# ScalarE and VectorE repeat 60 heads of a layer in loops, three heads a turn, beside TensorE

## The chip, the core and the metric

The kernel runs on one core of a Trainium2 chip. Its engines are TensorE (PE, with its weight loads as PEld), VectorE (DVE), ScalarE (ACT), GpSimd (POOL) and SyncE (SP), which issues all DMA transfers of tensors. The engines run on their own and wait for each other by semaphores. The metric is the time of one execution on the device in microseconds (us), lower is better.

## The reference, cut to what matters

Two layers, each an attention over a key-value cache and then a small mixer and MLP; one token for each of two batch entries. The weights are the same in both layers, and so are the caches: each layer reads all of K and V (2 x 32 heads x 16384 positions x 128, bfloat16, 268 MB each).

```python
def _A_ref(x, k_cache, v_cache, wq, wo):
    q = (x @ wq).reshape(B, Sq, H, Dh).transpose(0, 2, 1, 3)
    scores = jnp.einsum("bhqd,bhkd->bhqk", q, k_cache) * (Dh ** -0.5)
    p = _softmax(scores, axis=-1)
    o = jnp.einsum("bhqk,bhkd->bhqd", p, v_cache)
    return o.transpose(0, 2, 1, 3).reshape(B, Sq, H * Dh) @ wo
...
x = x + _A_ref(_layernorm(x), A_k_cache, A_v_cache, A_wq, A_wo)
x = x + _B_ref(_layernorm(x), B_w1, B_w2, B_w3, B_w4)
# and both lines once more
```

`_B_ref` is a layer norm, two 576x576 products around a shift along the sequence, and an MLP of 576 to 4608 to 576.

## The kernel before, in words

A "head" below is one of the U = 64 pairs of batch entry and head. K and V of one head are one tile each of 128 partitions x 32 KB (4 MB). The memory `mem` has six slots for such tiles; the plan in `plan_all` gives each tile its slot and its order in SP's queue: K of head s+1, then V of head s, and so on. The last two heads of the first layer and K of one more stay in memory and come first in the second layer (`order`, CARRY = 2). A transfer is issued when its slot is free: class `Store` records on which instructions it has to wait, and SP issues strictly in order (L98).

The whole program is recorded first as a list of operations per engine (class `Graph`); each names what it reads and writes, and `_waits` works out which other operations it must wait for, leaving out what another wait covers. `emit` then writes the engines' instructions. Operations of TensorE inside a range noted with `loop` are written once, as a hardware loop of turns; the waits of such a loop go to semaphores of its own (`own`), which each turn takes down again at its end (`_turn`). A loop cannot hold a wait for a DMA semaphore, whose value grows from turn to turn; so for TensorE, GpSimd waits for the tile (`landed`, `relay`, L177) and passes it on. VectorE and ScalarE are written out in full, instruction by instruction, for all heads, with one counting semaphore (`done`).

`attention` is the pass over heads, s = 0 to 63, each in eight chunks c (32 of the 64 blocks of each half of K go this way, `PB` = 32):

- TensorE transposes the eight blocks of chunk c (L852, into `tps`), ScalarE copies them out (L862, `kt`), and TensorE multiplies them with the query two chunks later (L872, scores into `sps`; LEAD = 2). So in chunk 0 of head s TensorE does the transposes of chunk 0 and the scores of chunk 6 of head s-1.
- VectorE does the other half of the scores itself, in four pieces at c = 0, 2, 4, 6: a product of K with the query in all partitions (L886, into `prod`) and a sum (L890, into `s_dve`). The first piece waits for the K tile's DMA.
- At c = 2 VectorE copies the output of head s-2 away (`keep_o`, L923) and takes the maxima of head s-1 (L897 to L901); GpSimd takes the maximum over partitions (L904); at c = 4 ScalarE writes the exponentials of head s-1 and their sums into columns of `l1` and `l2` (L912 to L917).
- From c = 4 to 7 TensorE multiplies the exponentials of head s-1 with V, a quarter at a time (`pv`, L941).
- At c = 6 the query of head s+1 is prepared: VectorE copies its column (L816) and scales a diagonal matrix with it (L818), TensorE spreads it over the partitions (L821), ScalarE copies it out (`qb`, L824).

After the last head `normalize` adds `l1` and `l2`, sums over partitions and scales the output; then come the products with wo, w3 and w4, whose weights take the places of the last tiles. In the first layer TensorE's loop is s = 1 to 60, in the second s = 4 to 63.

Of the kernel before, what the change touches and what calls it, by code (L numbers as in the profile page):

```python
# [16 lines left out]
class Op:  # L17


    __slots__ = ("eng", "fn", "deps", "waits", "needed", "own", "val", "sem", "sig", "pos", "know", "relay")  # L20

    def __init__(self, eng, fn, sig=None):
        self.eng, self.fn, self.sig = eng, fn, sig
        self.deps, self.waits = [], []
        self.needed = self.own = self.relay = False
        self.val = self.sem = self.know = None
# [6 lines left out]
class Graph:  # L33
# [5 lines left out]

    ENGS = ("sync", "scalar", "tensor", "vector", "gpsimd")  # L40

    def __init__(self, nc):
        self.nc = nc
        self.ops = {e: [] for e in self.ENGS}
        self.all = []
        self.writer = {}
        self.readers = {}
        self.dma_sems = {}
        self.dma_count = {}
        self.loops = []  # L50
# [25 lines left out]
    def op(self, eng, fn, reads=(), writes=(), sig=None):  # L76
        return self._add(Op(eng, fn, sig), reads, writes)
# [24 lines left out]

    def loop(self, first, turns):

        n = len(self.ops["tensor"]) - first
        assert n % turns == 0
        self.loops.append((first, n // turns, turns))
# [19 lines left out]
    def emit(self):  # L127
        nc = self.nc
        self._waits()
        pe = self.ops["tensor"]  # L130
        turn = {}
        for first, n, turns in self.loops:
            for i in range(first, first + n * turns):
                turn[i] = (first, n, (i - first) // n)
        for o in self.all:
            for d in o.waits:
                d.needed = True
                if o.eng == "tensor" and o.pos in turn and d.sem is None:
                    d.own = True
        for first, n, turns in self.loops:  # L140
            for i in range(n):
                same = [pe[first + i + n * t] for t in range(turns)]
                assert all(o.sig is not None and o.sig == same[0].sig for o in same), [o.sig for o in same]
                some = any(o.needed for o in same)
                for o in same:
                    o.needed = some
        done = {e: nc.alloc_semaphore(f"done_{e}") for e in self.ENGS if e != "sync"}
        own = {e: nc.alloc_semaphore(f"own_{e}") for e in self.ENGS if e not in ("sync", "tensor")}
        for o in self.all:
            if o.relay:  # L150
                o.own = o.needed = True
        for e in self.ENGS:
            n = {True: 0, False: 0}
            for o in self.ops[e]:
                if o.sem is None and o.needed:
                    n[o.own] += 1
                    o.val = n[o.own]
        for o in self.all:
            for d in o.waits:
                assert not d.own or o.eng == "tensor", (o.eng, d.eng)  # L160

        def wait(eng, need, seen):
            for (s, mine), v in need.items():
                if seen.get((s, mine), -1) < v:
                    eng.wait_ge(self.dma_sems[s] if s in self.dma_sems else (own if mine else done)[s], v)
                    seen[s, mine] = v

        def needs(o):
            need = {}
            for d in o.waits:  # L170
                k = (d.sem if d.sem is not None else d.eng, d.own)
                need[k] = max(need.get(k, 0), d.val)
            return need

        def emit_op(eng, e, o):
            if o.relay:
                eng.sem_inc(own[e], 1)  # L177
                return
            ins = o.fn(eng)
            if o.sem is None and o.needed:  # L180
                ins.then_inc((own if o.own else done)[e], 1)

        def runner(e):
            def run(eng):
                seen = {}
                for o in self.ops[e]:
                    wait(eng, needs(o), seen)
                    emit_op(eng, e, o)
            return run

        def run_pe(eng):
            seen, taken = {}, {}
            i = 0
            loops = {first: (n, turns) for first, n, turns in self.loops}
            while i < len(pe):
                if i in loops:
                    n, turns = loops[i]
                    taken = self._turn(eng, pe, i, n, turns, taken, wait, needs, emit_op, own)
                    seen = {k: v for k, v in seen.items() if not k[1]}
                    i += n * turns  # L200
                    continue
                o = pe[i]
                need = {k: v - (taken.get(k[0], 0) if k[1] else 0) for k, v in needs(o).items()}
                wait(eng, need, seen)
                emit_op(eng, "tensor", o)
                i += 1

        with nc.Block() as block:
            for e, sect in (("sync", block.sync), ("scalar", block.scalar), ("tensor", block.tensor),
                            ("vector", block.vector), ("gpsimd", block.gpsimd)):  # L210
                if self.ops[e]:
                    sect(run_pe if e == "tensor" else runner(e))

    def _turn(self, eng, pe, first, n, turns, taken, wait, needs, emit_op, own):

        table = [[needs(pe[first + t * n + i]) for i in range(n)] for t in range(turns)]
        assert all(k[1] for row in table for need in row for k in need), "a wait that no loop can hold"
        top = [{} for _ in range(turns)]
        for t, row in enumerate(table):
            for need in row:  # L220
                for (s, _), v in need.items():
                    top[t][s] = max(top[t].get(s, 0), v)
        step = {s: top[-1][s] - top[-2][s] for s in top[-1]}
        assert all(s in step for row in top for s in row)
        rel = []
        for i in range(n):
            need = {}
            for t in range(turns):
                for (s, m), v in table[t][i].items():
                    r = v - t * step[s] - taken.get(s, 0)  # L230
                    assert need.get((s, m), r) == r, (i, pe[first + i].sig, t, s, r, need)
                    need[s, m] = r
            rel.append(need)
        for s, v in step.items():
            assert max(need.get((s, True), 0) for need in rel) >= v, (s, v)
        me = eng.engine
        with self.nc.Fori(0, turns, 1, engines=OrderedEngineSet([me]), head_slot={me: 0}):
            seen = {}
            for i in range(n):
                wait(eng, rel[i], seen)  # L240
                emit_op(eng, "tensor", pe[first + i])
            for s, v in step.items():
                eng.sem_inc(own[s], -v)
        return {**taken, **{s: taken.get(s, 0) + v * turns for s, v in step.items()}}
# [60 lines left out]
class KB:  # L305
# [38 lines left out]
    def _alloc(self):  # L344
# [10 lines left out]
        self.qb = [sb(f"qb{i}", [128, 128], BF16) for i in range(2)]  # L355
        self.p = [sb(f"p{i}", [128, self.NB], BF16) for i in range(self.NS)]
        self.s_dve = [sb(f"s_dve{i}", [128, 2 * (self.BP - self.PB)], FP32) for i in range(2)]
        self.q_f = sb("q_f", [128, U], FP32)
        self.q_col = sb("q_col", [128, self.NS], BF16)
        self.mx = sb("mx", [128, 5, 4], FP32)  # L360
        self.l1 = sb("l1", [128, U], FP32)
        self.l2 = sb("l2", [128, U], FP32)
        self.o_acc = sb("o_acc", [128, U], FP32)
        self.otn = sb("otn", [128, U], BF16)
# [4 lines left out]
        self.rows = self.prod[:, 1024:1024 + self.D]  # L369
        self.x = sb("x", [128, KT, B], FP32)  # L370
# [10 lines left out]
        self.hg = [sb(f"hg{i}", [128, KT * NL * B], FP32) for i in range(2)]  # L381
# [110 lines left out]
    def dv(self, fn, reads=(), writes=()): return self.g.op("vector", fn, reads, writes)  # L492
    def act(self, fn, reads=(), writes=()): return self.g.op("scalar", fn, reads, writes)
# [55 lines left out]
    def layer(self, l):  # L549
# [6 lines left out]
        self.rows_projection("wo", l, lambda k: self.otn[:, k * self.B:(k + 1) * self.B], "otn")  # L556
# [182 lines left out]
    def attention(self, l):  # L739
        U, LEAD, NS = self.U, self.LEAD, self.NS  # L740
        o = self.order(l)
        pe = self.g.ops["tensor"]
# [3 lines left out]
        enter = self.CARRY + 2 if l else 1  # L746
        leave = enter + NS * ((U - enter) // NS)
        leave = min(leave, U) if l else leave - NS
# [4 lines left out]
        for s in range(U + 1):  # L753
            if s == enter:
                first = len(pe)
            if s == leave:
                self.g.loop(first, (leave - enter) // NS)
            if s < U and not self.kept(l, s):
# [3 lines left out]
            for c in range(2 * n):  # L762
                h = c // n
                if s < U:
                    u = o[s]
                    self.transposes(l, s, u, c)
                    self.evacuate()
                    pend.append((s, u, c, self.chunk))
                    self.chunk += 1
                while pend and (len(pend) > LEAD or s == U):  # L770
                    self.scores(*pend.pop(0))
                if s < U:
                    if c == 0 and prompt and s >= 1:
                        self.q_broadcast(o[s + 1], s + 1)
                    if c % n in (0, 2):
                        self.dots(l, s, u, h, c % n // 2)
                    if c == 2 * n - 2 and not prompt and s + 1 < max(U, leave + 1):
                        self.q_broadcast(o[min(s + 1, U - 1)], s + 1)
# [8 lines left out]
                elif s >= 1:  # L787
                    if c == LEAD:
                        if s >= 2:
                            self.keep_o(s - 2, o[s - 2])  # L790
                        self.softmax_max(l, s - 1, o[s - 1])
# [5 lines left out]
            if prompt:  # L797
                while pend:
                    self.scores(*pend.pop(0))
                if s >= 1:  # L800
                    self.keep_o(s - 1, o[s - 1])
                self.softmax_max(l, s, o[s])
        self.keep_o(U - 1, o[U - 1])
# [10 lines left out]
    def q_broadcast(self, u, s):  # L814
        i = s % self.NS
        self.dv(lambda e: e.tensor_copy(out=self.q_col[:, i:i + 1], in_=self.q_f[:, u:u + 1]),  # L816
                reads=["q_f"], writes=[("q_col", i)])
        self.dv(lambda e: e.tensor_scalar(out=self.diag[:, :], in0=self.ident[:, :], scalar1=self.q_f[:, u:u + 1],  # L818
                                          scalar2=None, op0=ALU.mult), reads=["ident", "q_f"], writes=["diag"])
# [230 lines left out]
```

## Time and profile before

| | |
|---|---|
| time, median of 3 runs | 2573.72 us (2573.01 to 2574.47) |
| profiled execution, own time | 2572.36 us |
| its span, first to last instruction | 2570.6 us |
| granted TensorE clock, mean | 0.571 |
| busy: PE, DVE, ACT, POOL | 63%, 74%, 47%, 6% |
| DMA: bytes, mean rate over the span | 1097 MB, 427 GB/s |
| K tile, V tile: median time from issue to landing | 41.2 us, 49.9 us |

The page cuts the span into 40 slices of 64 us and gives busy shares and DMA rate for each. The sum of waits tells for each engine and line what it waited for ("us in total, times, longest us"). In a timeline the columns are start, length, engine, line, operation, output and input, count, and in brackets the idle time ahead of it with what ended it. "SPq" is an instruction that SP issues. The length of an SP row that stands for several transfers is from the first to the last of them.

### The profile page before, as it was taken

The page shows a single profiled execution, that of the slowest core. Times are in us where ns is not written, and L with a number is a line of the kernel's source. Part 1 is how long each engine was busy: PE and PEld are TensorE (multiplying, and loading weights), DVE is VectorE, ACT ScalarE, POOL GpSimd, SP SyncE. Part 2 cuts the span into 40 slices and gives each one's busy share as a digit, 9 for nine tenths or more (in the row PEclk, how much of TensorE's full clock was granted, in tenths as well). Part 3 has the DMA queues.
Part 4 walks back from the last instruction along what each step waited for, and adds up shares of the span by engine and source line. Part 5 has one row for each costly group of instructions (what it writes and reads, how often), then busy time and mean ns, then how long its engine had stood idle before and what let it go on. Part 6 is the DMA issues. An engine that isn't in the chain of part 4 may idle for free.

```text
span 2570.6 us, 73557 instructions
## 1 busy us (share of the span) xinstructions
PE 1612.5 (63%) x34309; PEld 1575.9 (61%) x34309; DVE 1897.4 (74%) x1920; ACT 1203.8 (47%) x1816; POOL 158.9 (6%) x149
## 2 busy tenths in 40 slices
PE   4666566666656666666667766666666665666665
PEld 4666566666656656565557766656666665665665
DVE  5877777776777777678559977777777777777773
ACT  3544444444544444454335554444454444444442
POOL 0000000000000000000000000000000000000000
PEclk8555555555565555555556555555555555555555
DMA  9999999999999999999999999999999999999999
GB/s 408 431 432 431 430 432 431 431 431 433 431 431 433 432 432 432 432 432 430 389 405 430 431 431 431 432 432 432 432 432 431 431 432 432 431 432 431 431 421 349
DMA packets 58873, 1097.27 MB, mean 427 GB/s; under 512 B 4778, under 2 KB 23342, under 8 KB 23854
## 3 DMA queue, kind: packets, MB, share of 16 engines
q1 hardware_dynamic: 58798, 1096.33, 99.9%
q8 instruction: 40, 0.66, 0.1%
q14 instruction: 35, 0.29, 0.0%
HBM read 1096.30 MB, written 0.00 MB: 426 GB/s over the span
## 4 chain that ended last, share of the span: by engine, by line
DMA 66%; DVE 26%; PE 5%; issue 2%; SPq 0%; ACT 0%; DVEq 0%; POOL 0%; POOLq 0%
DMA mem<-in_A_k_cache_dram 60%; DVE s_dve L890 16%; DVE prod L886 9%; DMA mem<-in_A_v_cache_dram 4%; PE mps L941 2%; PE tps L852 2%; DMA mem<-in_B_w_dram 1%; DMA mem<-in_A_wo_dram 1%; PE sps L821 1%; SPq L98 0%; DMA mem<-in_A_wq_dram 0%; DVE diag L818 0%; PE sps L629 0%; PE mps L700 0%; DVE mx L901 0%
## 5 line engine op out<-in xcount | busy, mean ns | idle before, releaser
L862 ACT ACTIVATE kt<-tps 128x1024 bf16<-128x1024 bf16 x1026 | 1036.9, 1024 | 885.9 <-PE tps L852 868.8
L890 DVE TENSOR_REDUCE s_dve<-prod 128x16 f32<-128x2048 bf16 x512 | 1168.3, 2282 | 17.6
L852 PE MATMUL tps<-ident,mem 128*128 128x128 bf16 x8208 | 1001.8, 300 | 181.1 <-POOLq L177 178.2
L886 DVE TENSOR_TENSOR prod<-mem,qb 128x2048 bf16<-128x2048 bf16 x512 | 625.4, 1221 | 544.7 <-DMA mem<-in_A_k_cache_dram 528.7
L941 PE MATMUL mps<-p,mem 128*128 128x1 bf16 x16384 | 514.7, 165 | 599.7 <-ACT p L917 524.3
L852 PEld LDWEIGHTS tps<-ident,mem 128*128 128x128 bf16 x8208 | 763.7, 136 | 191.0 <-POOLq L177 187.8
L941 PEld LDWEIGHTS mps<-p,mem 128*128 128x128 bf16 x16384 | 487.0, 104 | 610.7 <-ACT p L917 590.7
L872 PEld LDWEIGHTS sps<-q_col,kt 128*128 128x128 bf16 x8208 | 411.6, 113 | 5.1 <-ACT kt L862 4.9
L872 PE MATMUL sps<-q_col,kt 128*128 128x1 bf16 x8208 | 400.4, 170 | 3.3 <-ACT kt L862 2.5
L904 POOL PARTITION_ALL_REDUCE mx<-mx x128 | 156.7, 1224 | 2356.3 <-DVE mx L901 2356.3
L912 ACT ACTIVATE mx<-mx 128x1 f32<-128x1 f32 x128 | 26.0, 203 | 324.1 <-POOL mx L904 324.1
L821 PE MATMUL sps<-diag,ones_bf 128*128 128x128 bf16 x129 | 37.0, 287 | 115.0 <-DVE diag L818 115.0
L821 PEld LDWEIGHTS sps<-diag,ones_bf 128*128 128x128 bf16 x129 | 13.5, 105 | 125.6 <-DVE diag L818 125.6
L824 ACT ACTIVATE qb<-sps 128x128 bf16<-128x128 f32 x129 | 35.7, 277 | 61.9 <-PE sps L821 61.8
L914 ACT ACTIVATE p<-s_dve,mx 128x64 bf16<-128x64 f32 x128 | 44.5, 348 | 4.2
L917 ACT ACTIVATE p<-sps,mx 128x64 bf16<-128x64 f32 x128 | 37.5, 293 | 0.0
L593 ACT ACTIVATE rstd<-rstd,eps 128x2 f32<-128x2 f32 x8 | 2.4, 296 | 67.5 <-DVE rstd L591 67.5
L923 DVE COPY o_acc<-mps 128x1 f32<-128x1 f32 x128 | 19.1, 149 | 19.3 <-PE mps L941 19.3
L818 DVE TENSOR_SCALAR diag<-ident,q_f 128x128 bf16<-128x128 bf16 x129 | 31.7, 245 | 0.3 <-PE sps L821 0.3
L899 DVE TENSOR_REDUCE mx<-sps 128x1 f32<-128x64 f32 x128 | 27.6, 216 | 2.6 <-PE sps L872 2.4
L680 DVE TENSOR_TENSOR x<-x,mps 128x8 f32<-128x8 f32 x4 | 0.7, 164 | 38.4 <-PE mps L700 38.4
L897 DVE TENSOR_REDUCE mx<-s_dve 128x1 f32<-128x64 f32 x128 | 26.8, 209 | 0.0
(90 smaller groups left out, 218.0 us busy)
## 6 DMA issues: line engine op xcount, KB each, us to landing
mem<-in_A_v_cache_dram SPq DMA_DIRECT2D x124, 4096.0 KB, 49.9
mem<-in_A_k_cache_dram SPq DMA_DIRECT2D x122, 4096.0 KB, 41.2
mem<-in_B_w_dram SPq DMA_DIRECT2D x13, 1152.0 KB, 12.8
mem<-in_A_k_cache_dram SPq DMA_DIRECT2D x7, 2048.0 KB, 14.7
mem<-in_A_wq_dram SPq DMA_DIRECT2D x8, 1024.0 KB, 8.9
mem<-in_A_v_cache_dram SPq DMA_DIRECT2D x4, 2048.0 KB, 22.1
mem<-in_A_wo_dram SPq DMA_DIRECT2D x4, 1584.0 KB, 29.8
mem<-in_B_w_dram SPq DMA_DIRECT2D x6, 576.0 KB, 10.9
```

What stands on the lines that cost most here:

```text
L818: self.dv(lambda e: e.tensor_scalar(out=self.diag[:, :], in0=self.ident[:, :], scalar1=self.q_f[:, u:u + 1], scalar2=None, op0=ALU.mult), ...
L821: self.pe(lambda pe: pe.matmul(qps, lhsT=self.ones_bf[:, :], rhs=self.diag[:, :], start=True, stop=True, skip_group_check=True), reads=["o ...
L824: self.act(lambda e: e.activation(out=self.qb[s % 2][:, :], in_=qps, func=ACT.Copy), reads=[("qps", i)], writes=[("qb", s % 2)])
L852: ins = pe.transpose(self.tps[t][:, j * 128:(j + 1) * 128], buf[:, j * 128:(j + 1) * 128], self.ident[:, :])
L862: self.act(lambda e: e.activation(out=self.kt[k][:, :, :], in_=self.tps[t][:, :].rearrange("p (i c) -> p i c", i=self.CH), func=ACT.Copy), ...
L872: ins = pe.matmul(self.sps[sp][:, c * self.CH + j:c * self.CH + j + 1], lhsT=self.kt[k][:, j, :], rhs=self.q_col[:, sp:sp + 1], start=True ...
L886: self.dv(lambda e: e.tensor_tensor(out=prod, in0=buf.rearrange("p (j d) -> p j d", d=128), in1=qbc, op=ALU.mult), reads=[("qb", s % 2)] + ...
L890: self.dv(lambda e: e.tensor_reduce(out=sd[:, c0:c0 + DB], in_=prod, axis=AX.X, op=ALU.add), reads=["prod"], writes=[("s_dve", s % 2)])
L904: self.pool(lambda e: e.partition_all_reduce(self.mx[:, 3, m:m + 1], self.mx[:, 2, m:m + 1], channels=128, reduce_op=ROP.max), reads=[("mx ...
L914: self.act(lambda e: e.activation(out=p[:, n:self.NB], in_=self.s_dve[s % 2][:, 0:self.NB - n], func=ACT.Exp, bias=self.mx[:, 4, m:m + 1], ...
L917: self.act(lambda e: e.activation(out=p[:, 0:n], in_=self.sps[i][:, 0:n], func=ACT.Exp, bias=self.mx[:, 4, m:m + 1], scale=self.scale, acc ...
L941: ins = pe.matmul(self.mps[:, 448:449], lhsT=buf[:, j * 128:(j + 1) * 128], rhs=p[:, col:col + 1], start=(h == 0 and b == 0), stop=(h == 1 ...
```

## The change

Loops are kept for ScalarE and VectorE as for TensorE. Each operation in a loop has a signature (`sig`), so that the three turns' heads are seen to be alike, and where it reads or writes a column that moves with the head, the column (`col`) is formed from the turn's number: the query's column, the column of `o_acc`, and that of `l`. Each consumer engine's loop has semaphores of its own (`tensor_vector` is what VectorE's loop waits for from TensorE). To make all heads alike and all waits ones that a loop can hold:

- the buffers `qb`, `s_dve` and `mx` go by three instead of two or four;
- the first product of VectorE in a looped head (`go`) no longer waits for the tile's DMA but for TensorE's scores at c = 0, that is of chunk 6 of the head before, which stand behind the first transposes of this head;
- a K tile in a loop is given free with the scores issued at c = 7 (`of`, scores of chunk 5), which stand behind all of VectorE's products of the head by way of the query's matrix, instead of with the last transposes;
- the two sums of exponentials of a head are added by VectorE in the loop (`keep_l`, behind `keep_o`), both after the maxima, and `normalize` has one addition less; in the second layer one column is copied home at the end;
- the loop of the first layer is s = 2 to 61 for all three engines; that of the second stays s = 4 to 63.

Some scratch arrays now lie in `prod` and `kt`. The core of the diff:

```diff
+    LOOPED = ("tensor", "scalar", "vector")
...
+    def mark(self):
+        return {e: len(self.ops[e]) for e in self.LOOPED}
+
     def loop(self, first, turns):
 
-        n = len(self.ops["tensor"]) - first
-        assert n % turns == 0
-        self.loops.append((first, n // turns, turns))
+        for e, i in first.items():
+            n = len(self.ops[e]) - i
+            assert n % turns == 0, (e, n, turns)
+            self.loops[e][i] = (n // turns, turns)
...
-        with self.nc.Fori(0, turns, 1, engines=OrderedEngineSet([me]), head_slot={me: 0}):
+        with self.nc.Fori(0, turns, 1, engines=OrderedEngineSet([me]), head_slot={me: 0}) as turn:
             seen = {}
             for i in range(n):
                 wait(eng, rel[i], seen)
-                emit_op(eng, "tensor", pe[first + i])
-            for s, v in step.items():
-                eng.sem_inc(own[s], -v)
-        return {**taken, **{s: taken.get(s, 0) + v * turns for s, v in step.items()}}
+                o = ops[first + i]
+                emit_op(eng, o, None if o.col is None else turn * (ops[first + n + i].col - o.col) + o.col)
+            for k, v in step.items():
+                eng.sem_inc(handle(k), -v)
+        return {**taken, **{k: taken.get(k, 0) + v * turns for k, v in step.items()}}
...
-        enter = self.CARRY + 2 if l else 1
+        enter = self.CARRY + 2 if l else 2
         leave = enter + NS * ((U - enter) // NS)
-        leave = min(leave, U) if l else leave - NS
+        leave = min(leave, U) if l else leave
...
-                first = len(pe)
+                first = self.g.mark()
...
+            turning = enter <= s < leave
+            if l and s == U:
+                self.home()
...
+                end = turning and c == 2 * n - 1
                 if s < U:
                     u = o[s]
-                    self.transposes(l, s, u, c)
-                    self.evacuate()
+                    self.transposes(l, s, u, c, hold=turning and c % n == n - 1)
+                    self.evacuate(s, c)
...
-                    self.scores(*pend.pop(0))
+                    self.scores(*pend.pop(0), go=turning and c == 0, of=(l, o[s]) if end else None)
...
-                        self.dots(l, s, u, h, c % n // 2)
+                        self.dots(l, s, u, h, c % n // 2, go=turning and c == 0)
...
+                        self.softmax_max(l, s - 1, o[s - 1])
                         if s >= 2:
-                            self.keep_o(s - 2, o[s - 2])
-                        self.softmax_max(l, s - 1, o[s - 1])
+                            self.keep(l, s - 2)
...
+        reads, writes = [("q_col", sp), ("kt", k)], [("sps", sp)]
+        if go:
+            writes = writes + ["go"]
+        last = []
+        if of:
+            for h in range(2):
+                nm, _, keys = self.tile(of[0], "k", of[1], h * self.BP, self.BP)
+                reads = reads + keys
+                last.append(nm)
+        self.pe(f, reads=reads, writes=writes, sig=("s", c, k, sp, go, of is not None))
+        for nm in last:
+            self.used(of[0], nm, self.CH)
...
-                reads=[("qb", s % 2)] + keys, writes=["prod"])
+                reads=[("qb", r)] + keys + (["go"] if go else []), writes=["prod"], sig=("mult", r, c0, keys[0]))
...
+    def keep(self, l, s):
+
+        i = s % self.NS
+        self.dv(lambda e, c: e.tensor_copy(out=self.o_acc[:, bass.ds(c, 1)], in_=self.mps[:, 448:449]),
+                reads=["ops"], writes=["o_acc"], sig="keep_o", col=self.place(l, s))
+        self.dv(lambda e, c: e.tensor_tensor(out=self.l[:, bass.ds(c, 1)], in0=self.ls[:, 0, i:i + 1],
+                                             in1=self.ls[:, 1, i:i + 1], op=ALU.add),
+                reads=[("ls0", i), ("ls1", i)], writes=["l"], sig=("keep_l", i), col=self.place(l, s))
```

As built, VectorE's loop body is three heads with three register operations a head, and ends with three semaphore operations, a register addition and a compare-and-branch; ScalarE's likewise without the column work.

## The prediction

> **What bounds the kernel now.** I read the page first (slices, queues), then the sum of waits, then the order of the built instructions with their waits, then the timeline at three places: a head in steady state, the heads just after the layer change, and the last two heads.
>
> ```profile
> span 2570.6 us, 73557 instructions
> GB/s 408 431 432 431 430 432 431 431 431 433 431 431 433 432 432 432 432 432 430 389 405 430 431 431 431 432 432 432 432 432 431 431 432 432 431 432 431 431 421 349
> q8 instruction: 40, 0.66, 0.1%
> q14 instruction: 35, 0.29, 0.0%
> DVE prod L886 <- DMA mem<-in_A_k_cache_dram: 528.7, 114, 8.4
> ```
>
> Outside the start, the layer change and the end, DMA moves 431 to 433 GB/s in every slice, and VectorE waits 4.6 us per head (528.7/114) for its K tile. So the stream of tiles sets the time: one head starts every 19.43 us (from 2428.31 to 2486.60 are three heads, 58.29 us). What compute needs per head is read where VectorE is behind, after the layer change. There it starts a head every 15.60 us (1396.05, 1411.65, 1427.24, 1442.83), so it has 3.8 us of cover:
>
> ```profile
> 1395.12 0.24 DVE L818 TENSOR_SCALAR diag<-ident,q_f 128x128 bf16<-128x128 bf16 x1
> 1395.42 0.29 PE L821 MATMUL sps<-diag,ones_bf 128*128 128x128 bf16 x1 [0.91 <-DVE diag L818]
> 1395.50 1.04 PE L941 MATMUL mps<-p,mem 128*128 128x1 bf16 x32
> 1396.05 1.23 DVE L886 TENSOR_TENSOR prod<-mem,qb 128x2048 bf16<-128x2048 bf16 x1 [0.69 <-ACT qb L824]
> 1396.40 1.01 PE L852 MATMUL tps<-ident,mem 128*128 128x128 bf16 x8
> 1397.21 0.40 PE L872 MATMUL sps<-q_col,kt 128*128 128x1 bf16 x8
> 1397.47 0.99 PE L941 MATMUL mps<-p,mem 128*128 128x1 bf16 x32
> 1398.32 1.01 PE L852 MATMUL tps<-ident,mem 128*128 128x128 bf16 x8
> 1399.13 0.40 PE L872 MATMUL sps<-q_col,kt 128*128 128x1 bf16 x8
> 1430.17 1.04 PE L852 MATMUL tps<-ident,mem 128*128 128x128 bf16 x8 [0.53 <-issue]
> ```
>
> This is one head boundary. VectorE ends a head with diag. TensorE then does q (L821), the third part of pv (L941), the last transposes of this head (L852, 1396.40), scores of chunk 5 (L872), the last part of pv, the first transposes of the next head (1398.32) and scores of chunk 6 (1399.13). VectorE runs beside this: at 1396.05, 0.69 us after diag, it is already in the next head. The last row is the same first transposes where TensorE jumps back in its loop.
>
> **What the change adds: go.** In a loop VectorE cannot wait for a tile's own semaphore. Its first product of each looped head now waits for a signal of TensorE, that of the scores of chunk 6 of the head before, the last but one row of the boundary. These end at 1399.53; a start after a wait of this kind takes 0.09 us (K lands at 2428.22 in the chain, product at 2428.31). So the product of 1396.05 would start at 1399.62, 3.57 us later. At the two boundaries that follow the difference is 3.57 (1442.83) and 4.25 (1427.24: TensorE's jump costs 0.66 there; at 1476.65 it costs 0.36). VectorE and TensorE, which ran side by side across the boundary, now run one after the other.
>
> Compute per head: 15.60 + 3.57 + 0.17 (one jump of 0.51 in three heads) + 0.07 (one new addition per head, keep_l; its neighbour keep_o starts 0.07 before the next instruction) = 19.40 us. The tiles need 19.43. The cover of 3.8 us is used up to the last 0.03.
>
> The new register work, three operations per head that form column addresses, is shown by no row. Below: nothing, since each can be done while VectorE is in a product or sum of 1.22 to 2.29 us. Above: the jump of TensorE, with its register work, costs 0.36 to 0.66, so 0.15 each, 0.45 per head. I take nothing, by the row that is nearest: keep_o starts 0.08 before the sum ahead of it ends, so VectorE's queue is filled ahead. The jumps of VectorE and ScalarE: VectorE's lies inside the 4.2 us from diag to go and would have to exceed that; ScalarE's stands before the evacuation of chunk 0, which is wanted only three matmul groups later, and TensorE stands idle 4.7 us later in each head anyway (590.7 over 126, for p). I cost both at nothing; a jump as dear as entering the loop (2.16 idle at 1382.90) would still be covered.
>
> [...]
>
> **What it removes.** (1) VectorE's and ScalarE's unrolled code. In twelve heads the K tile lands late by up to 0.98 us (584.63 starts 20.39 after its forerunner instead of 19.43), seven times in the first layer (5.7 us in all) and five in the second (3.1). The page counts 75 packets of code loading; if these are the cause, they go. Below: nothing. I take 5 for the first layer (some of it is caught at the change) and nothing for the second, where compute decides. (2) One addition per layer before the normalization, 0.2 us; the two copies of home() take about that back.
>
> **First layer.** VectorE began pass s=2 at 58.95. With go and TensorE's entry into the loop, which now falls here (2.2 us), it is 64.7. Fifty-eight passes of 19.40 lead to 1189.9 for s=60, which started at 1189.87 before. Then s=61 starts at 1209.3; s=62 and 63 are outside the loop, at 15.60 each, 1224.9 and 1240.5, ahead of the tiles that they waited for (1228.82, 1249.22). So nothing is lost at the layer change and the 5 us are kept.
>
> **Second layer.** Here is the price. Pass s=4 (1380.46) is the first of the loop: its go ends at 1383.73 + 0.40, so 1384.2; less the 5 us, 1379.2. In before VectorE was 24 us behind the stream here and worked that off at 3.8 us a head until 1492.59. With 19.40 against 19.43 it works off nothing: s=62 starts at 1379.2 + 58 x 19.40 = 2504.4 instead of 2486.60, late by 17.8. DMA isn't short of places by that in between: a K tile took 41.2 us from issue to landing, so a release 27 us later still leaves 14, over the 9.7 of one tile.
>
> **The end.** In the last heads a place for w1 and all behind it in SP's queue (V of the last two heads, wo, w3, w4) comes free with K of s=62:
>
> ```profile
> 2486.60 1.23 DVE L886 TENSOR_TENSOR prod<-mem,qb 128x2048 bf16<-128x2048 bf16 x1 [4.53 <-DMA mem<-in_A_k_cache_dram]
> 2498.98 1.26 SPq L98 DMA_DIRECT2D mem<-in_B_w_dram  x3
> 2503.35 0.40 PE L872 MATMUL sps<-q_col,kt 128*128 128x1 bf16 x8
> ```
>
> Before, SP waited for VectorE's fourth product, 12.4 us after the head's start. Now it waits for the scores of chunk 5 (2503.35), 17.2 after it. At 2499 some 0.75 MB were still on their way (25.1 MB move from then to the end, 24.4 of them new), 1.7 us, and 0.9 us were lost in a dip; the new work began, as it were, at 15.0 after the start. Now DMA runs dry first, and the rate needs about 2 us to come back after an issue: 19.2. So 4.2 us more.
>
> Sum: 17.8 + 4.2 = 22.0 on the profiled execution's 2572.36 gives 2594.4. The median stands 1.4 above it: 2596.
>
> **Rivals.**
> - A, as summed, with compute at 19.30 to 19.50 per head: at 19.30 the first layer gains 5.5 and s=62 starts at 2498.1, total 2589; at 19.50 s=63 of the first layer starts 2.8 us early instead of 5, s=62 of the second at 2512.4, total 2604. Chance 0.50.
> - B, register work or waits show: at 19.60 the first layer ends 3 us late, s=62 starts at 2524, total 2615; at 19.85 2645. For it: three operations per head that no row prices. Against: the queue that is filled ahead. Chance 0.28.
> - C, the serial path is shorter than I read, 18.9 to 19.2 per head (granted clock: all transposes at the boundary took 1.01, those at full clock take 0.61, so up to 0.8 us): the backlog goes down, total 2572 to 2583. Against: the clock comes up only some 7 us into a busy stretch (1402.59), past go. Chance 0.13.
> - D, on the other side, not slower: go costs TensorE's first transposes alone (1.2 us), because the cover of 3.8 us is enough at all times, and code loading no longer delays tiles: -8.8 + 1.2 + 0 to 4.2 at the end, 2567 to 2572 by the median. It decides where compute per head is under about 18.9. For it: the late tiles above. Against: the boundary rows. Chance 0.09.
>
> **How the numbers follow.** The likeliest is A, 2596; its own range is 2589 to 2604. The slope is 58 us per us of compute time in the second layer, and twice that once the first layer falls behind too. The range 2577 to 2632 holds A, the lower half of C and B up to 19.75: about 0.8. 0.2% (5.1 us) is about what a measurement of this kernel can tell from no change. Faster by more needs the best of D: 0.05. Within it lie the rest of D and half of C: 0.09. Slower: 0.86.
>
> **What would show it.** Right: idle time before VectorE's product is put down to TensorE's scores, not to DMA; heads start every 19.4 us in both layers; after the layer change VectorE's idle time does not shrink and DMA's rate in the last two slices falls, since w1 is issued some 22 us later after the last K tile has long landed; the instruction queues carry fewer packets. B would show as gaps around keep_l or diag, D as products that start 1.2 us after landing with the second layer in step by 1500. The forecast is wrong if heads in the second layer start clearly faster than every 19.3 us or slower than 19.5.

## The result, and the profile after

The changed kernel takes 2596.79 us (median; 2596.15 to 2597.68), the one before 2573.97 on the same chip: a ratio of 1.0089 (95% interval 1.0072 to 1.0107), slower by 22.8 us. The forecast was 2596. The profiled execution took 2597.14 us, its span is 2595.4, 24.8 longer than before. In the page of the profile, the span, the DMA rate by slices, the two code-loading queues and the first line of the chain that ended last:

```profile
span 2595.4 us, 74490 instructions
GB/s 405 428 432 431 432 431 431 432 432 432 432 431 432 431 432 431 432 432 432 396 422 418 426 429 433 430 432 430 433 431 429 434 429 433 429 432 431 433 242 363
q8 instruction: 40, 0.66, 0.1%
q14 instruction: 13, 0.11, 0.0%
DVE 61%; PE 21%; issue 13%; DMA 3%; SPq 1%; DVEq 0%; ACT 0%; POOL 0%; POOLq 0%
```

Up to the layer change (slice 20) the rate is what it was. The hole is in the last slice but one: 242 GB/s where 421 stood (the last has 363 for 349), because SP could not issue w1 and what follows until a K tile came free, 27.7 us later than before, where it issued w1 at 2498.98:

```profile
2526.70 1.25 SPq L100 DMA_DIRECT2D mem<-in_B_w_dram  x3
```

The forecast had the rate fall in both of the last slices and w1 come some 22 us later. The chain that ended last is now VectorE's and TensorE's work in turn; DMA has 3% of it, where it had 66%. The sum of waits says what VectorE's products wait for:

```profile
DVE prod L943 <- PE sps L917: 529.9, 120, 8.0
```

120 waits are all the looped heads of both layers, and none of them is for a tile any more. The timeline at a head boundary just after the layer change (columns: start, length, engine, line, operation, in brackets the idle time before it and what ended it):

```profile
1395.62 0.24 DVE L860 TENSOR_SCALAR diag<-ident,q_f 128x128 bf16<-128x128 bf16 x1
1395.93 0.29 PE L864 MATMUL sps<-diag,ones_bf 128*128 128x128 bf16 x1 [2.04 <-DVE diag L860]
1396.01 1.04 PE L1001 MATMUL mps<-p,mem 128*128 128x1 bf16 x32
1396.91 1.01 PE L895 MATMUL tps<-ident,mem 128*128 128x128 bf16 x8
1397.71 0.40 PE L917 MATMUL sps<-q_col,kt 128*128 128x1 bf16 x8
1397.97 0.99 PE L1001 MATMUL mps<-p,mem 128*128 128x1 bf16 x32
1398.83 1.01 PE L895 MATMUL tps<-ident,mem 128*128 128x128 bf16 x8
1399.63 0.40 PE L917 MATMUL sps<-q_col,kt 128*128 128x1 bf16 x8
1400.14 1.23 DVE L943 TENSOR_TENSOR prod<-mem,qb 128x2048 bf16<-128x2048 bf16 x1 [4.27 <-PE sps L917]
```

VectorE ends its head with diag, stands still for 4.27 us while TensorE works through seven groups, and goes on 0.11 us after the last of them. Before, it was back at work 0.69 us after diag. In the second layer a head starts every 19.33, 19.33 and 19.72 us (the third holds TensorE's jump): 58.39 a turn, 19.46 a head from the first loop turn to the last. So the 24 us that VectorE is behind the stream after the layer change are never worked off.

Head starts (VectorE's first product), us:

| | before | forecast | after |
|---|---|---|---|
| first layer, s=2 | 58.95 | 64.7 | 66.95 |
| s=60 | 1189.87 | 1189.9 | 1195.86 |
| s=63 | 1249.22 | 1240.5, tiles allowing (5 early) | 1246.60 (2.6 early) |
| second layer, s=4 | 1380.46 | 1379.2 | 1380.81 |
| s=62 | 2486.60 | 2504.4 | 2509.36 |
| s=62 to end of span | 84.0 | 88.2 | 86.0 |

### The profile page after: what moved, and what is told of

Same layout as the page of the kernel before. It is cut to its first block, busy times and chain, and to the rows that moved or that the text cites. A ratio compares the mean times of both kernels' runs of the same rounds, so it can differ in the third digit from the quotient of the medians.

```text
span 2595.4 us, 74490 instructions
## 1 busy us (share of the span) xinstructions
PE 1598.9 (62%) x34309; PEld 1568.2 (60%) x34309; DVE 1916.8 (74%) x2048; ACT 1205.5 (46%) x1816; POOL 51.5 (2%) x149
## 4 chain that ended last, share of the span: by engine, by line
DVE 61%; PE 21%; issue 13%; DMA 3%; SPq 1%; DVEq 0%; ACT 0%; POOL 0%; POOLq 0%
DVE s_dve L947 33%; DVE prod L943 23%; PE tps L895 9%; PE mps L1001 8%; PE sps L917 2%; SPq L100 1%; PE sps L864 1%; DMA mem<-in_A_k_cache_dram 1%; DMA mem<-in_B_w_dram 1%; DVE diag L860 1%; DVE l L982 1%; DVE mx L956 1%; DVE q_col L857 1%; DVE mx L954 1%; DMA mem<-in_A_wo_dram 1%
## 5 line engine op out<-in xcount | busy, mean ns | idle before, releaser
L895 PE MATMUL tps<-ident,mem 128*128 128x128 bf16 x8208 | 998.2, 299 | 21.5 <-issue 13.1
L960 POOL PARTITION_ALL_REDUCE mx<-mx x128 | 49.3, 385 | 2487.8 <-DVE mx L958 2411.8
L723 PE MATMUL mps<-prod,mem 128*128 128x2 bf16 x680 | 20.7, 165 | 23.5 <-DMA mem<-in_B_w_dram 14.1
L723 PEld LDWEIGHTS mps<-prod,mem 128*128 128x128 bf16 x680 | 19.4, 104 | 25.0 <-DMA mem<-in_B_w_dram 12.2
```

The source lines that it names most:

```text
L723: ins = pe.matmul(self.mps[:, t * B:(t + 1) * B], lhsT=buf[:, o:o + 128], rhs=rhs(k), start=(k == 0 and t == 0), stop=(k == last), skip_gr ...
L895: ins = pe.transpose(self.tps[t][:, j * 128:(j + 1) * 128], buf[:, j * 128:(j + 1) * 128], self.ident[:, :])
L960: self.pool(lambda e: e.partition_all_reduce(mx[3], mx[2], channels=128, reduce_op=ROP.max), reads=[("mx2", i)], writes=[("mx3", i)])
```

## The experiments

Theory S, that of the forecast: the signal go puts VectorE behind TensorE at each head boundary, so compute takes as long as the stream of tiles, and the backlog of the layer change stays. Theory L: the loops themselves cost (jumps, register work, additional semaphores). Theory R: K tiles come free too late and DMA starves. Each run was compared with the kernel before on its own chip (medians 2573.14 to 2573.36).

**e1: go alone, in the kernel before.**

```diff
-                    self.scores(*pend.pop(0))
+                    self.scores(*pend.pop(0), go=turning and c == 0)
...
-                        self.dots(l, s, u, h, c % n // 2)
+                        self.dots(l, s, u, h, c % n // 2, go=turning and c == 0)
...
-        self.pe(f, reads=[("q_col", sp), ("kt", k)], writes=[("sps", sp)], sig=("s", c, k, sp))
+        self.pe(f, reads=[("q_col", sp), ("kt", k)], writes=[("sps", sp)] + (["go"] if go else []), sig=("s", c, k, sp, go))
...
-                reads=[("qb", s % 2)] + keys, writes=["prod"])
+                reads=[("qb", s % 2)] + keys + (["go"] if go else []), writes=["prod"])
```

> The kernel before, with one edit: in the heads of TensorE's loop VectorE's first product also waits for TensorE's scores of chunk 6 (go). VectorE and ScalarE stay written out, K's release, buffers and sums stay as before. Theory S (serial): the wait alone puts VectorE behind TensorE at each head boundary, so compute takes 15.60 + 3.57 + 0.13 = about 19.3 us a head, the backlog of 24 us after the layer change is hardly worked off, s=62 of the second layer starts near 2503, and the time is 2588 (2584 to 2592). Theory L (the loops of VectorE and ScalarE, their jumps and register work, cost the time) and theory R (late release of K starves DMA): nothing of theirs is in this kernel, 2574 (2572 to 2577).

Measured: 2588.51 us, ratio 1.0055 (1.0039 to 1.0072). Heads of the second layer start every 19.31 us, s=62 at 2505.92. Its sum of waits:

```profile
DVE prod L887 <- PE sps L873: 533.6, 120, 5.5
```

With VectorE and ScalarE still written out in full, and K released as before, the wait alone brings 15.4 of the 22.8 us, at the place and in the number that S names. L and R have no part in this kernel. What the kernel after has beyond it can be read between the two profiles: s=62 starts 3.4 us later (58 heads with 0.15 more each, less the 5.2 by which s=4 starts earlier), and from there to the end it takes 4.6 us more (86.0 against 81.4), as w1 is issued 17.3 instead of 12.4 us after the head's start.

**e2: all loops, without go.** GpSimd, which waits for the K tile anyway, tells VectorE's loop too.

```diff
-                self.landed(l, "k", o[s])
+                self.landed(l, "k", o[s], dve=turning)
...
-                    self.scores(*pend.pop(0), go=turning and c == 0, of=(l, o[s]) if end else None)
+                    self.scores(*pend.pop(0), of=(l, o[s]) if end else None)
...
+            if dve:
+                self.g.relay([k for nm in some for k in self.store.keys(nm)], ["go"], "vector")
```

> The kernel after, with the signal go taken from TensorE and given to GpSimd: GpSimd, which waits for the K tile's landing for TensorE already, tells VectorE's loop too, on a semaphore of its own. Loops of all three engines, register work, keep_l and the late release of K stay. Theory S: VectorE runs beside TensorE again, compute is under 16 us a head, the backlog is worked off at over 3 us a head, s=62 of the second layer starts at or up to 9 us before 2486.6 (code loading no longer delays tiles), and the late release costs 2 to 4 us at the end: 2566 to 2574. Theory L and theory R: as the kernel after, 2595 (2590 to 2599).

Measured: 2566.68 us, ratio 0.9974 (0.9963 to 0.9985), 30 us less than after and 6.5 less than before. In its sum of waits and its timeline at a boundary after the layer change:

```profile
DVE prod L945 <- POOLq L201: 482.5, 111, 4.6
```

```profile
1389.76 0.24 DVE L862 TENSOR_SCALAR diag<-ident,q_f 128x128 bf16<-128x128 bf16 x1
1390.69 1.23 DVE L945 TENSOR_TENSOR prod<-mem,qb 128x2048 bf16<-128x2048 bf16 x1 [0.69 <-ACT qb L869]
```

VectorE waits for the tile again (by way of GpSimd's queue, L201), and where it is behind it goes on 0.69 us after diag, as before the change. Compute is 15.75 us a head against 15.60 before: all three loops, with jumps and register work, cost 0.15, and seven heads after s=4 the heads are in step with the stream, one every 19.43 us to the end. L and R fall as causes of the loss: the loops of all three engines and the late release are in this kernel.

**e3: late release alone, in the kernel before.**

```diff
-                    self.transposes(l, s, u, c)
+                    self.transposes(l, s, u, c, hold=turning and c % n == n - 1)
...
-                    self.scores(*pend.pop(0))
+                    self.scores(*pend.pop(0), of=(l, o[s]) if turning and c == 2 * n - 1 else None)
```

> The kernel before, with one edit: in the heads of TensorE's loop a K tile is given free with the scores of chunk 5 instead of the last transposes and VectorE's last product, as in the kernel after. Theory S (VectorE and TensorE in series at the head boundary make the loss): heads still start every 19.43 us once the layer change is made up for, s=62 of the second layer near 2486.6, and only the end is later, since w1 waits for a scores group 5 us later: 2574 to 2578. Theory R (late release starves DMA): most of the 23 us, 2590 to 2597.

Measured: 2574.86 us, ratio 1.0006 (0.9996 to 1.0015); 1.5 us over before, which the interval does not tell from nothing. Heads start every 19.43 us, s=62 at 2487.47; from there to the end it takes 85.85 us instead of 84.05. The place of the 1.8 us is that named, and R gets no more than this where the tiles keep DMA busy to the end. In the kernel after, where DMA has run dry by then as in e1, w1 is issued 4.9 us later than in e1 and the end takes 4.6 more; so there the late release is the likely cause of 4.6 us.

**e4 and e7: the same additional VectorE operation, in the kernel after and in e2.**

```diff
     def q_broadcast(self, u, s):
...
+        self.dv(lambda e: e.tensor_copy(out=self.diag[:, :], in_=self.ident[:, :]), reads=["ident"], writes=["diag"], sig="extra")
```

> The kernel after, with one more VectorE operation per head: the identity is copied into diag (128x128 bf16) just before diag is written, some 0.1 to 0.25 us on the path from the last sum to the query's matrix. Theory S: compute at 19.46 a head is already at the stream's 19.43, so the whole addition shows in each head of the second layer, and in the first layer less the 2.6 us by which its last head is early now: for 0.15 us a head 58 x 0.15 + (58 x 0.15 - 2.6) = 14.8, 2611; for 0.25 us 26, 2623; range 2605 to 2624. Theory D (the stream of tiles still paces, and the 23 us are lost in DMA after late release): VectorE's addition is covered, 2597 (2595 to 2599).

> The kernel e2 (VectorE told of the landing by GpSimd) with the same additional VectorE operation per head as in e4, which showed 0.24 us there and cost 27 us. Theory S: compute at about 15.75 + 0.24 = 16.0 us a head stays 3.4 under the stream's 19.43, so the operation is covered but for the heads that make up for the layer change: at most 1 us, 2566 to 2569. If VectorE's work counted in each head whatever the waits (theory L): 2566.7 + 58 x 0.24 or more, 2580 to 2594.

Measured in e4: 2624.23 us, ratio 1.0198 (1.0181 to 1.0215), 27.4 over after. Heads start every 19.70 us instead of 19.46, in both layers. Measured in e7: 2567.07 us, ratio 0.9976 (0.9965 to 0.9986), 0.4 over e2; compute where VectorE is behind is 15.98 instead of 15.75, and in step the heads start every 19.43 all the same. The same operation, 0.23 to 0.24 us per head in both, costs 27 us where compute is as long as the stream and nothing measurable where it has 3.5 us of cover.

**e9: one group of TensorE moved behind go.** The last part of pv goes behind the scores that signal; three heads are written out for it.

```diff
-        enter = self.CARRY + 2 if l else 2
+        enter = self.CARRY + 2 + NS if l else 2
...
+                if c == 0 and enter <= s <= leave:
+                    self.pv(l, s - 2, o[s - 2], 3)
...
-                        self.pv(l, s - 1, o[s - 1], 2 * c - 3)
+                        if c == 2 or s != enter - 1:
+                            self.pv(l, s - 1, o[s - 1], 2 * c - 3)
...
-                    if 0 <= c - n < 4:
+                    if 0 <= c - n < 4 - (enter - 1 <= s < leave):
```

> The kernel after, with TensorE's order changed at the boundary alone: the last part of pv of a head (0.99 us of matmuls) goes behind the first transposes and the scores of chunk 6, so go comes one pv part earlier. The first three looped heads of the second layer are written out for it (its loop is s=7 to 63). Theory S: compute falls to 19.46 - 0.99 = 18.5 us a head, nearly 1 us under the stream's 19.43; over 57 heads that is more than the 24 us of backlog, less 11 us by the three heads written out, so VectorE is back in step before the end and the time is 2568 to 2577. Theory L or R: the order of TensorE's work changes neither the loops nor the release, 2590 to 2597 (only the three heads written out can help, by 11 us at most: 2586).

Measured: 2568.51 us, ratio 0.9980 (0.9971 to 0.9990). Its timeline at a looped boundary:

```profile
1442.38 0.40 PE L920 MATMUL sps<-q_col,kt 128*128 128x1 bf16 x8
1442.64 0.99 PE L1004 MATMUL mps<-p,mem 128*128 128x1 bf16 x32
1442.89 1.23 DVE L946 TENSOR_TENSOR prod<-mem,qb 128x2048 bf16<-128x2048 bf16 x1 [3.42 <-PE sps L920]
```

VectorE's idle time falls from 4.27 to 3.42 us, and heads start every 18.49 us, 0.97 less. (The rest, 0.12, is TensorE's jump, which no longer shows: the three heads of a turn take 18.48, 18.48 and 18.50.) 0.9 us a head under the stream is enough to work off the backlog: from s=22 on heads start every 19.43, and s=62 starts at 2480.59. So 28 us went with one group of 32 matmuls moved, of which the three heads written out can have at most 11. The loops, their jumps, the register work and the late release are still there.

**e6: keep behind a long operation.**

```diff
+                    if turning and c == 1:
+                        self.keep(l, s - 2)
...
-                        if s >= 2:
+                        if s >= 2 and not turning:
                             self.keep(l, s - 2)
```

> The kernel after, with keep_o and keep_l of the looped heads moved from behind the maxima (between short operations) to behind VectorE's first sum (2.29 us long); no operation more or less. If the register operations that form their columns show because the operations ahead of them are too short, they hide behind the sum: compute falls from 19.46 by about 0.1 to 19.36 us a head, 58 x 0.1 in the second layer and the gain of the first by it where tiles allow: 2585 to 2592, and GpSimd's maximum over partitions, again beside VectorE's product from its start, goes back from 0.39 to about 1.2 us without cost. If the 0.17 are the plain cost of one more operation: 2595 to 2598.

Measured: 2583.46 us, ratio 1.0038 (1.0023 to 1.0052), 13.3 less than after; a head takes 19.24 us, 0.22 less, twice what was expected. The timeline of VectorE and GpSimd around the maxima, first of after, then of e6:

```profile
1407.56 0.16 DVE L958 TENSOR_TENSOR mx<-mx 128x1 f32<-128x1 f32 x1
1407.67 0.16 DVE L980 COPY o_acc<-mps 128x1 f32 x1
1407.78 0.16 DVE L982 TENSOR_TENSOR l<-ls 128x1 f32 x1
1407.81 0.35 POOL L960 PARTITION_ALL_REDUCE mx<-mx  x1 [18.98 <-DVE mx L958]
1407.86 1.22 DVE L943 TENSOR_TENSOR prod<-mem,qb 128x2048 bf16<-128x2048 bf16 x1
```

```profile
1401.98 0.15 DVE L982 COPY o_acc<-mps 128x1 f32 x1
1402.04 0.15 DVE L984 TENSOR_TENSOR l<-ls 128x1 f32 x1
1402.11 1.22 DVE L945 TENSOR_TENSOR prod<-mem,qb 128x2048 bf16<-128x2048 bf16 x1
...
1405.94 0.16 DVE L960 TENSOR_TENSOR mx<-mx 128x1 f32<-128x1 f32 x1
1406.02 1.22 DVE L945 TENSOR_TENSOR prod<-mem,qb 128x2048 bf16<-128x2048 bf16 x1
1406.19 1.25 POOL L962 PARTITION_ALL_REDUCE mx<-mx  x1 [17.86 <-DVE mx L960]
```

In after the product starts 0.30 us behind the last maximum, in e6 0.08: the two operations take 0.22 there. Behind a sum they are nearly free: from the sum's start to the next product it is 2.34 us with them (1399.77 to 1402.11) and 2.32 without (1407.27 to 1409.59). So the two operations cost 0.22 at the one place and next to nothing at the other. How much of that goes to the columns from registers can be read in the kernel after itself, where the last two heads of the first layer are written out, with fixed columns, and have the same operations at the same place:

```profile
1238.36 0.16 DVE L958 TENSOR_TENSOR mx<-mx 128x1 f32<-128x1 f32 x1
1238.43 0.15 DVE L980 COPY o_acc<-mps 128x1 f32<-128x1 f32 x1
1238.50 0.15 DVE L982 TENSOR_TENSOR l<-ls 128x1 f32<-128x1 f32 x1
1238.57 1.22 DVE L943 TENSOR_TENSOR prod<-mem,qb 128x2048 bf16<-128x2048 bf16 x1
```

Here the product starts 0.21 us behind the last maximum, in the loop 0.30. So some 0.13 of the 0.22 is the place behind short operations, whatever the column, and 0.09 comes with the column from a register. Behind the sum neither shows. That the 0.09 are the register operations that form the columns, hidden where the operation ahead is long, is the author's explanation: no row shows a register operation by itself.

**e5: e2 with the second layer's loop ended three heads earlier.**

```diff
-        leave = min(leave, U) if l else leave
+        leave = min(leave, U) - NS if l else leave
```

> The kernel e2 (loops of three engines, VectorE told of the landing by GpSimd), with the second layer's loop ended three heads earlier (s=4 to 60), so that the last three heads are written out and give K free with VectorE's last product, as before the change. e2 ended 6.5 us ahead of before although its last heads started 8.4 us ahead. If the late release costs these 1.9 us at the end: 2564.5 (2563 to 2566). If they come from elsewhere (wo, w3, w4, the tail): as e2, 2566.7.

Measured: 2564.64 us, ratio 0.9966 (0.9953 to 0.9978): 2.0 less than e2, and 8.7 less than before. From s=62 to the end it takes 84.67 us, in e2 86.76. The 2 us of late release are had back; this is the fastest version found.

**e8: six heads a turn.**

```diff
-                self.g.loop(first, (leave - enter) // NS)
+                self.g.loop(first, (leave - enter) // (2 * NS))
```

> The kernel after, with six heads in a loop's turn instead of three, on all three engines: half as many jumps, nothing else moved. In after two heads of a turn take 19.33 us and the one with TensorE's jump 19.72, so a jump costs 0.39 and a head 0.13 on the average. If that is the jump, compute falls by 0.065 to 19.39 us a head: 58 x 0.065 = 3.8 us in the second layer and up to 2.6 in the first, 2590 to 2593. If the 0.39 come from something else that recurs with three buffers (their addresses, their waits): as after, 2595 to 2598.

Measured: 2713.25 us, ratio 1.0546 (1.0531 to 1.0560), 116 us over after where a gain of 4 to 7 was expected. The five heads without a jump take 19.33 us each, as in after, and the one with the jump 26.1 to 27.2. From its queues, its waits and its timeline:

```profile
q8 instruction: 304, 4.98, 0.7%
```

```profile
PE tps L895 <- issue: 136.0, 20, 7.7
```

```profile
1559.42 1.03 PE L895 MATMUL tps<-ident,mem 128*128 128x128 bf16 x8 [7.05 <-issue]
```

At each of 20 loop entries or jumps TensorE stands for about 7 us with nothing to wait for that the profile shows, and 264 more packets of code of 16.4 KB are loaded, 13 a turn on the average. The turn has 6 x 257 = 1542 matmuls, each with a weight load. From these counts it is the author's estimate that the longer body is loaded anew in each turn; no row names the code that a packet holds. In after, with half of it, that queue has 40 packets as before, and TensorE's idle time at the first transposes of a looped head is 13.1 us in all. So the expectation on the jump could not be read from the time, but its first half can be read from the heads: those without a jump take 19.33, so the 0.39 of every third head in after is the jump's.

## Why the prediction was right, step by step

- **What bounds, and the price of go.** Right. The difference from diag to the product was forecast as 0.69 + 3.57 = 4.26 us, and is 4.26 (1415.21 to 1419.47). e1 shows the wait by itself, e2 its absence, e9 one matmul group of it.
- **Compute per head** was summed to 19.40 and is 19.46. Two terms are off. The jump: 0.39 a turn, 0.13 a head, for 0.17. keep_l with the register work: 0.17 a head (VectorE's head from first product to the end of diag 15.07 instead of 14.90), for 0.07 + 0. The 0.07 for keep_l was right, as the written-out heads at 1238.43 show. The step that failed is "each can be done while VectorE is in a product or sum", which put the register work at nothing: keep_o and keep_l stand behind the maxima, which are short, and there their register columns take 0.09. e6 gets all of the 0.22 back by moving both operations. The terms as given add up to 19.41, so the sum was 0.05 to 0.06 a head short; that is small, but it put compute above the stream's 19.43 instead of below.
- **First layer.** Forecast 5 us early at its end, measured 2.6. The entry into the loop at s=2 takes 3.6 us of TensorE, for 2.2 (s=2 starts 2.3 late), and 58 heads at 0.06 more are another 3.7; so s=63 came 6.1 after the 1240.5 that was forecast for it and ate half of the gain. The gain itself was right: e2 and e6, whose heads have room, end the layer 5.2 us early (1244.03 and 1243.99). In e2, e5, e7 and e9, from where VectorE has come into step and leaving out the last head of each layer, not one head starts later than 19.55 us after the last; counted so, before has twelve and e3, with the late release but VectorE's code written out, has nine. So the late tiles go with the written-out code. That its loading delays them is likely: 35 packets of code in queue 14 became 13 to 15, and the traces have one of these packets 15 to 17 us (mostly 16.1) ahead of eleven of the twelve late heads of before and of eight of the nine of e3, but at that distance ahead of only 5 of some hundred heads of before that are in time. How a packet of 8 KB makes a tile late by up to 0.98 us no run shows.
- **Second layer.** s=4 was forecast for 1379.2 and started at 1380.81. 58 heads at 19.46 take 1128.6 us for the 1125.2 forecast. Together 5.0 us later than forecast at s=62: 22.8 late instead of 17.8.
- **The end.** Forecast 4.2 us, measured 2.0. w1 was issued 17.3 us after the head's start, as forecast (17.2), against 12.4 before. The 2 us for the rate to come back are in the trace of after: w1 is issued at 2526.70, DMA moves nothing until 2527.70, 148 GB/s on the mean from there to 2528.95 and 493 in the 1.5 us that follow. What the sum left out is a slow stretch of before further on: from 27 to 39 us after w1's issue DMA moves 335 GB/s there (2525.98 to 2537.98) and 402 in after (2553.70 to 2565.70), by these rates an estimated 2.0 us of the 12. The 2 us and the slow stretch offset each other, so that the forecast's other terms, 17.2 - 15.0 = 2.2, come near the 2.0 measured. e1 has the early w1 and a DMA that has run dry as in after: from w1's issue to the end it takes 69.0 us, after 68.7 and before 71.6, and from s=62 to the end 81.4, 2.7 less than before, which had the 1.7 + 0.9 still to move or lost.
- **The sum.** +5.0 at s=62 and -2.2 at the end are the 2.8 by which the span grew more than forecast, a tenth of a per cent. The two have opposite signs, and the medians grew by 22.8 us where the profiled executions grew by 24.8. So the bound, the price of go and the backlog were right, but that the time came within 1 us of 2596 is luck: its terms were off by 2 to 5 us.
- **The rivals.** B was half right in kind: 0.09 a head come with the columns from registers, not 0.2 to 0.45. C and D fall by the boundary rows: the transposes there take 1.01 us in after too. (C's "only some 7 us into a busy stretch" holds at 1402.59 alone, where the granted clock is 0.50 up to 1403.0 and 0.95 in the 0.5 us behind it; in before the transposes already take 0.61 at 1386.11, 3.2 us after TensorE set out at 1382.90.) (D's own terms add up to 2566 to 2570, not 2567 to 2572.) But D's first term was real: without go (e2) s=62 starts 8.4 us earlier than before, for D's 8.8, and 2.7 of it go at the end.

## What to carry to other kernels

Here a wait that moved from a transfer to another engine's signal cost what that engine had queued ahead of the signal, 3.6 us a head (4.27 of idle time for 0.69): read these rows at the boundary, add them to the compute time per step, and compare the sum with the pace of the stream, because a backlog is worked off only by the difference (3.8 us a head before, nothing in after, 0.9 in e9). Where a loop holds no wait for a DMA semaphore, as in this kernel, let an idle engine relay the landing to each consumer rather than chain the consumers (e2: 30 us less than the kernel after). And look at how many instructions a loop body has before making it longer (e8: about 7 us at an entry or jump with 1542 matmuls in a turn, 0.39 at a jump in after with 771).

## What the runs showed that had not been expected

- The loop body of six heads cost TensorE about 7 us at every entry or jump (e8: 136.0 us over 20), the one of three heads 0.39 (after).
- GpSimd's maximum over partitions takes 0.39 us on the average in after and 1.22 in before. It is the place of keep: in e6, where the product again starts 0.08 us behind the maximum, it is 1.23. In after it starts 0.05 us ahead of VectorE's product (1407.81) and is done in 0.35, and the product takes its usual 1.22; in e6 it starts 0.17 behind the product and ends 0.20 after the product's end (1407.44 against 1407.24). Why it is longer behind the product's start no run shows. The shorter maximum was no gain here, as TensorE waited for VectorE and not for the maximum.
- keep_o and keep_l cost about 0.11 us each with a column from a register and 0.07 with a fixed one where they stand behind the maxima (after), and about 0.01 with the register column behind a sum of 2.29 us (e6).
- A code packet of 8 KB in queue 14 stands 15 to 17 us ahead of nearly every late tile in before and in e3.
